# Ordering the first group's fp16 splits behind the next copy out of PSUM, and pulling one attention unit ahead of a weight transpose

## The chip, the cores and the metric

The kernel runs on 1 core of one Trainium2 chip. The metric is the device time of one execution in microseconds (us). Before the change it is 954.72 us, the median of 3 runs (952.37 to 956.6). Below, PE is TensorE, DVE is VectorE, ACT is ScalarE, POOL is GpSimd, SP is SyncE.

## What is computed

A decaying linear attention, then a gated block without an activation function, then a mixture of 8 experts in which each token goes to its two best ones:

```
for t in range(S):                                # B, H, S, D = 4, 8, 768, 48
    state = alpha[t][:, None] * state + outer(k[t], v[t])
    y[t]  = q[t] @ state
x   = y as 3072 tokens x 384
h   = ((x @ w1) * (x @ w2)) @ w3                  # 384 -> 1024 -> 1024
x   = h @ w_out                                   # 1024 -> 384
logits = x @ w_gate + log1p(exp(x @ w_noise)) * noise
out = sum over the top 2 experts e of  weight * (relu(x @ ew1[e]) @ ew2[e])
```

All of it is float32 in and out.

## The kernel before

Tokens are handled in 8 groups of G = 384 (three blocks of 128). Large products are done in fp16 with each float32 operand cut into a high and a low half by `split`: ACT writes `hi` (line 180), then DVE or POOL writes `lo = src - hi` (lines 182 and 184); three matmuls (high times high, high times low, low times high) stand for one.

**Stages.** Attention is a list of small units (`att_units`): `prep_*` (transposes of q, k, alpha and their scaling, lines 219 to 246), `scores` (L299), the masking of the scores (L316), `mix` (L342 and L353: query times state, scores times v), `ktok` (L330), `state` (L374 to L386), `xturn` (L407, with the copy L408 into `xT`). The gated block and the weights are another list (`mix_units`): `wide` (L541 to L543) makes one block of 128 columns of x@w1 (i = 0) or x@w2 (i = 1) in PSUM; ACT copies it out as `ab0` or `ab1` (L545); after the second, DVE multiplies the two (L551) and `split` makes `gh` and `gl`. `narrow` (L570 to L572) multiplies those by the 1024 x 400 matrix W = w3 @ [w_out, w_out@gates]. W itself is made during the first group, by `fuse_units`: for each of 8 row blocks of w_out, `fuse_out_turn` (three transposes, L482, and ACT's copy `woT`, L484) and `fuse_out` (L490); then for 16 half blocks of w3, `fuse_turn` (four transposes, L499, split into `w3h` and `w3l`) and `fuse_mul` (twelve matmuls, L510 to L512). Weights come as 64-bit words that `conversions` turns into float32 on DVE and ACT (L422, L424, L427).

After attention come routing (`rank`) and the experts (L922 to L934). Weights of the first experts are prepared beside the last `wide` and `narrow` units: `EARLY` lists how many preparing steps go behind each unit that is left once attention has ended.

**What sets the order.** PE's order is written out by the main loop: it emits one attention unit, adds its cost to `ta`, and then emits units of the other list as long as their summed cost `tm` stays under a limit that grows with `ta`. Each unit of both lists carries a cost, in estimated us. On the other engines a scheduler orders the instructions; `tc.issue_after(i)` makes an instruction stand behind instruction `i`. The engines then take their own instructions strictly in the order of their queue.

For groups 1 to 7 and blocks f < 7, the split of a gated block isn't emitted at once: it is kept in `AB["rest"]`, and at the next `wide` it is emitted with `behind=copied.ins`, so that ACT's `gh` stands behind the next copy `ab`. In group 0, and for f = 7, it is emitted at once.

Of the kernel before, what the change touches and what calls it, by code (L numbers as in the profile page):

```python
# [13 lines left out]
AF = mybir.ActivationFunctionType  # L14
# [12 lines left out]
NF = F // P  # L27
# [17 lines left out]
RG = 6  # L45
WB = 12
WU = 3
WP = 3
TA = 30
CS = 2.6  # L50
# [9 lines left out]
PGL = range(4)  # L60
# [21 lines left out]
def body(ctx, tc, q, k, v, alpha, mw1, mw2, mw3, mwo, wg, wn, noise, ew1, ew2, out, dbg=None):  # L82
    nc = tc.nc
# [92 lines left out]
    def split(src, hi, lo, scale=None, engine=None, behind=None):  # L176
        with ExitStack() as st:
            if behind is not None:
                st.enter_context(tc.issue_after(behind))
            nc.scalar.activation(hi, src, AF.Copy, scale=1.0 if scale is None else scale)  # L180
        if scale is None:
            (engine or nc.vector).tensor_tensor(lo, src, hi, OP.subtract)  # L182
        else:
            nc.vector.scalar_tensor_tensor(lo, src, scale, hi, op0=OP.mult, op1=OP.subtract)  # L184
# [20 lines left out]
    def bank(*shape, dt=F32):  # L205

        t = ps.tile([P, PB], F32, name="ps")
        if dt != F32:
            t = t.bitcast(dt)
        n = 1  # L210
        for x in shape:
            n *= x
        t = t[:, :n]
        return t if len(shape) == 1 else t.rearrange("p (a b) -> p a b", a=shape[0])
# [218 lines left out]
    FT, FO, FS = {}, {}, {}  # L433
# [44 lines left out]
    def fuse_out_turn(f):  # L478
        wo = FS.pop(f)
        tr = bank(NK, P)  # L480
        for kk in range(NK):
            nc.tensor.transpose(tr[:, kk, :], wo[:, kk * P:(kk + 1) * P], ident)  # L482
        FO[f] = stg.tile([P, NK, P], F32, name="woT")
        nc.scalar.activation(FO[f], tr, AF.Copy)  # L484

    def fuse_out(f):
        woT = FO.pop(f)
        pr = bank(2 * E)
        for kk in range(NK):
            nc.tensor.matmul(pr, woT[:, kk, :], wr[:, kk, :], start=kk == 0, stop=kk == NK - 1)  # L490
        split(pr, woh[:, f, DM:], wol[:, f, DM:], SW)

    def fuse_turn(f, hf):
        s = FS.pop((f, hf))
        th = stg.tile([P, 4, P], F16, name="w3h", bufs=3)
        tl = stg.tile([P, 4, P], F16, name="w3l", bufs=3)
        tr = bank(4, P)
        for j in range(4):
            nc.tensor.transpose(tr[:, j, :], s[:, j * P:(j + 1) * P], ident)  # L499
        split(tr, th, tl, SW)  # L500
        FT[f, hf] = (th, tl)

    def fuse_mul(f, hf):
        th, tl = FT.pop((f, hf))
        if hf == 0:
            FT[f] = bank(W)
        pw = FT[f]
        for j in range(4):
            kk = 4 * hf + j
            nc.tensor.matmul(pw, th[:, j, :], woh[:, kk, :], start=kk == 0, stop=False)  # L510
            nc.tensor.matmul(pw, th[:, j, :], wol[:, kk, :], start=False, stop=False)
            nc.tensor.matmul(pw, tl[:, j, :], woh[:, kk, :], start=False, stop=kk == NF - 1)  # L512
        if hf:
            split(FT.pop(f), Wf[0][:, f], Wf[1][:, f], 1.0 / SW)
# [3 lines left out]
    GS, AB, X2, RT, LAST = {}, {}, {}, {}, []  # L518
# [13 lines left out]
    def wide(g, f, i, c1=G):  # L532

        xT = XT[g]
        fs = slice(f * P, (f + 1) * P)
        c0 = GS.get((g, f, i), 0)
        GS[g, f, i] = c1
        cs, n = slice(c0, c1), c1 - c0
        pm = bank(n)
        for kk in range(NK):  # L540
            nc.tensor.matmul(pm, wab[i][0][:, kk, fs], xT[:, kk, cs], start=kk == 0, stop=False)  # L541
            nc.tensor.matmul(pm, wab[i][0][:, kk, fs], xT[:, NK + kk, cs], start=False, stop=False)  # L542
            nc.tensor.matmul(pm, wab[i][1][:, kk, fs], xT[:, kk, cs], start=False, stop=kk == NK - 1)  # L543
        a = gp.tile([P, G], F32, name=f"ab{i}")[:, :n]
        copied = nc.scalar.activation(a, pm, AF.Copy, scale=SG if i == 0 else 1.0)  # L545
        if "rest" in AB:
            split(*AB.pop("rest"), behind=copied.ins)
        AB[i] = a
        if i:
            a = AB[0]  # L550
            nc.vector.tensor_tensor(a, AB[1], a, OP.mult)  # L551
            if c0 == 0:
                GS[g, f] = [gp.tile([P, G], F16, name=x, bufs=10) for x in ("gh", "gl")]
            gh, gl = GS[g, f]
            if 0 < g and f < NF - 1:
                AB["rest"] = (a, gh, gl)
            else:
                split(a, gh[:, cs], gl[:, cs], engine=nc.gpsimd if g == 0 and f in PGL else None)

    def narrow(g, t, part):  # L560
        ts = slice(t * P, (t + 1) * P)
# [219 lines left out]
    def fuse_units():  # L781

        n0 = 4 * NK
        yield 0.33, (lambda: fuse_out_turn(0)), n0 + 1
        for f in range(NF - 1):
            yield 0.33, (lambda f=f: fuse_out_turn(f + 1)), n0 + f + 2
            yield 0.55, (lambda f=f: fuse_out(f)), 0
        n0 += NF
        seq = [(f, hf) for f in range(NF) for hf in range(2)]
        yield 0.45, (lambda: fuse_turn(*seq[0])), n0 + 1  # L790
        yield 0.55, (lambda: fuse_out(NF - 1)), 0
        for n, x in enumerate(seq):
            if n + 1 < len(seq):
                yield 0.45, (lambda n=n: fuse_turn(*seq[n + 1])), n0 + n + 2
            yield 2.05, (lambda x=x: fuse_mul(*x)), 0
# [16 lines left out]
    def mix_units():  # L812
        fu = fuse_units()
        for g in range(NG):
            for f in range(NF):
                for i in range(2):
                    if g == 0:
                        yield (0.0, (lambda f=f: convert((f // 4 + 1) * 2 * NK + AH)), TG - 1)
                    yield (1.48, (lambda g=g, f=f, i=i: wide(g, f, i)), (g + 1) * TG - 1)
                    if g == 0 and f >= FF:  # L820
                        c, x, n = next(fu)
                        yield 0.0, (lambda n=n: convert(n + AH)), 0
                        yield c, x, 0
                if f == (RF if g == NG - 1 else RG) and g:
                    yield (0.1, (lambda g=g: LAST.append(rank(g - 1))), 0)
                if g == NG - 1 and 0 <= f - NF + NTP[0] < NTP[0]:
                    yield (0.0, (lambda t=f - NF + NTP[0]: turn_part(0, 0, t)), 0)
            if g == 0:
                for c, x, n in fu:
                    yield 0.0, (lambda n=n: convert(n + AH)), 0  # L830
                    yield c, x, 0
                yield (0.0, end_of_weights, 0)
            for t in range(TG):
                for part in range(2):
                    yield (2.05, (lambda g=g, t=t, part=part: narrow(g, t, part)), 0)
# [352 lines left out]
    def warm(n):  # L1188

        pm = bank(HF) if n else None  # L1190
        for _ in range(n):
            nc.tensor.matmul(pm, ident16, idle, start=True, stop=True)
# [5 lines left out]
    with tc.manual_schedule(engines={mybir.EngineType.PE}):  # L1198
# [4 lines left out]
        for c, f in att_units():  # L1203
            turned = set(done)
            f()
            ready |= turned
            ta += c
            if MS not in done:
                t0 = ta
                dve = [i for i in nc.cur_bb.bb.instructions[-40:] if i.engine == mybir.EngineType.DVE]  # L1210
                marks += dve[-1:]
                if marks:
                    with tc.issue_after(marks[max(0, len(marks) - LAG)]):
                        convert(int(CR * (ta - CS)))
                if c and 0 in done and nconv >= 2 * NK and pieces:
                    wide(0, *pieces.pop(0), P)
                elif c:
                    warm(WP if ta < 4.1 else WU)
                continue
            while nxt is not None and nxt[2] in ready | {0} and tm < RATIO * (min(ta, TK) - t0) + R2 * max(ta - TK, 0.0):  # L1220
                nxt[1]()
                tm += nxt[0]
                nxt = next(M, None)
# [42 lines left out]
```

## Time and profile before

| | |
|---|---|
| time, median of 3 runs | 954.72 us (952.37 to 956.6) |
| time of the profiled execution | 952.11 us |
| its span | 950.4 us |
| PE busy | 915.6 us (96%) |
| PE weight loads busy | 602.1 us (63%) |
| DVE busy | 621.2 us (65%) |
| ACT busy | 449.4 us (47%) |
| POOL busy | 255.6 us (27%) |
| mean granted PE clock | 0.983 of full speed |

The span is the stretch from the first to the last instruction on the chip; the execution's time is 1.7 us longer. Busy shares are averages over stages of different kinds: the first 200 us hold the weights and the first group, the attention runs to 482 us (last L407), the experts from 529.4 us (first L922). The clock row of the page tells in tenths what part of PE's full speed was granted in each of 40 slices of 23.8 us.

### The profile page before, as it was taken

Reading aid. Unit: us, or ns where it says so; the run is one execution under the profiler, and the core shown is the slowest. Engines: PE = TensorE matmul, PEld = TensorE weight load, DVE = VectorE, ACT = ScalarE, POOL = GpSimd, SP = SyncE. Lnnn points to the kernel's source line nnn. Section 1 sums busy time; section 2 is a strip of 40 time slices with the busy share of each in tenths; the row PEclk is TensorE's granted clock in tenths of the full one; section 3 lists DMA queues with packets and bytes.
Section 4 is the critical chain, followed back from the end, with each engine's and each line's share of the span. In section 5 each row is a group of like instructions: output and inputs, shape, how many; then the busy total and the mean of one; then the engine's idle time right before and its main releaser. Section 6 shows DMA issues by size and latency. Waiting matters only on the chain.

```text
span 950.4 us, 17655 instructions
## 1 busy us (share of the span) xinstructions
PE 915.6 (96%) x6823; PEld 602.1 (63%) x6823; DVE 621.2 (65%) x1705; ACT 449.4 (47%) x908; POOL 255.6 (27%) x246
## 2 busy tenths in 40 slices
PE   7889999999999999999999999999999999999996
PEld 4667777777766666676665456656656565656563
DVE  6988878577879798696878836636272635545220
ACT  2676666363565655645555432334342524334321
POOL 1211110003141231415052162542323242333213
PEclk9979799999999999999999999999999999999999
DMA  9889672242405344101137267975857565776313
GB/s 241 230 151 137 162 186 64 42 84 80 96 15 115 42 108 60 65 4 44 59 111 148 92 125 177 188 153 142 142 123 155 120 153 100 173 127 136 37 11 45
DMA packets 189269, 105.54 MB, mean 111 GB/s; under 512 B 156912, under 2 KB 174912, under 8 KB 189184
## 3 DMA queue, kind: packets, MB, share of 16 engines
q1 hardware_dynamic: 172624, 68.04, 33.9%
q0 software_dynamic: 16560, 36.37, 17.9%
q8 instruction: 54, 0.88, 0.4%
q14 instruction: 31, 0.25, 0.1%
HBM read 73.06 MB, written 20.31 MB: 98 GB/s over the span
## 4 chain that ended last, share of the span: by engine, by line
PE 69%; DVE 19%; ACT 6%; issue 3%; DMA 1%; another core or an unknown queue 0%; POOL 0%; POOLq 0%; DVEq 0%; ACTq 0%; SPq 0%
PE ps L922 7%; PE ps L932 7%; PE ps L924 6%; PE ps L923 6%; PE ps L933 6%; PE ps L934 6%; PE ps L541 3%; PE ps L543 3%; PE ps L542 3%; PE ps L353 2%; PE ps L570 2%; PE ps L572 2%; PE ps L571 2%; PE ps L299 2%; DVE Gx L235 1%
## 5 line engine op out<-in xcount | busy, mean ns | idle before, releaser
L926 DVE SCALAR_TENSOR_TENSOR hl<-ps,hh 128x512 f16<-128x512 f32 (+1 forms) x128 | 74.2, 587 | 101.6 <-ACT hh L925 101.1
L923 PE MATMUL ps<-xT,eh 128*128 128x320 f16 (+1 forms) x384 | 130.3, 339 | 0.0
L924 PE MATMUL ps<-xT,el 128*128 128x320 f16 (+1 forms) x384 | 130.3, 339 | 0.0
L922 PE MATMUL ps<-xT,eh 128*128 128x320 f16 (+1 forms) x384 | 130.3, 339 | 0.0
L958 POOL DMA_INDIRECT out_dram<-ysb,mt x56 | 86.9, 1551 | 154.4 <-ACT ysb L955 152.6
L933 PE MATMUL ps<-el,hh 128*128 128x384 f16 x384 | 125.3, 326 | 0.0
L934 PE MATMUL ps<-eh,hl 128*128 128x384 f16 x384 | 125.3, 326 | 0.0
L932 PE MATMUL ps<-eh,hh 128*128 128x384 f16 x384 | 125.3, 326 | 0.0
L925 ACT ACTIVATE hh<-ps 128x512 f16<-128x512 f32 (+1 forms) x128 | 65.6, 516 | 101.8 <-PE ps L924 92.4
L955 ACT ACTIVATE ysb<-ps,wv 128x384 f32<-128x384 f32 (+1 forms) x56 | 32.4, 578 | 142.1 <-PE ps L934 80.3
L184 DVE SCALAR_TENSOR_TENSOR el<-es,esc,eh 128x512 f16<-128x512 f32 (+1 forms) x80 | 67.1, 856 | 43.5 <-ACT eh L180 37.4
L700 POOL DMA_INDIRECT table<-md,ad x48 | 50.8, 1058 | 155.4 <-DVE ad L697 127.2
L910 POOL DMA_INDIRECT xg<-x2s,mt x56 | 54.9, 981 | 104.6 <-DMA mt<-table 67.5
L545 ACT ACTIVATE ab<-ps 128x384 f32<-128x384 f32 (+2 forms) x136 | 62.9, 470 | 38.2 <-PE ps L543 20.2
L182 POOL TENSOR_TENSOR sm<-sf,sm 128x512 f16<-128x512 f32 x24 | 29.9, 1272 | 154.2 <-ACT sm L180 154.2
L541 PE MATMUL ps<-xT,w1h 128*128 128x384 f16 (+2 forms) x204 | 65.1, 321 | 1.0 <-DVE Kt L246 0.6
L570 PE MATMUL ps<-Wh,gh 128*128 128x400 f16 x192 | 63.9, 333 | 1.8 <-ACT gh L180 1.5
L541 PE MATMUL ps<-xT,w0h 128*128 128x384 f16 (+2 forms) x204 | 64.6, 319 | 1.1 <-ACT xT L408 1.1
L543 PE MATMUL ps<-xT,w1l 128*128 128x384 f16 (+2 forms) x204 | 65.1, 320 | 0.2 <-DVE w1l L184 0.2
L542 PE MATMUL ps<-xT,w1h 128*128 128x384 f16 (+2 forms) x204 | 65.1, 320 | 0.0
L543 PE MATMUL ps<-xT,w0l 128*128 128x384 f16 (+2 forms) x204 | 64.6, 319 | 0.0
L542 PE MATMUL ps<-xT,w0h 128*128 128x384 f16 (+2 forms) x204 | 64.5, 318 | 0.0
(288 smaller groups left out, 2072.9 us busy)
## 6 DMA issues: line engine op xcount, KB each, us to landing
es<-in_moe_w_dram SPq DMA_DIRECT2D x32, 768.0 KB
s<-in_moe_w_dram POOLq DMA_DIRECT2D x16, 512.0 KB
out_dram<-zero POOLq DMA_DIRECT2D x5, 960.0 KB
v<-in_v_dram SPq DMA_DIRECT2D x24, 192.0 KB
x2s<-xr SPq DMA_DIRECT2D x24, 192.0 KB
pad<-in_alpha_dram SPq DMA_DIRECT2D x21, 192.0 KB
pad<-in_q_dram SPq DMA_DIRECT2D x21, 192.0 KB
pad<-in_k_dram SPq DMA_DIRECT2D x21, 192.0 KB
```

What stands on the lines that cost most here:

```text
L541: nc.tensor.matmul(pm, wab[i][0][:, kk, fs], xT[:, kk, cs], start=kk == 0, stop=False)
L542: nc.tensor.matmul(pm, wab[i][0][:, kk, fs], xT[:, NK + kk, cs], start=False, stop=False)
L543: nc.tensor.matmul(pm, wab[i][1][:, kk, fs], xT[:, kk, cs], start=False, stop=kk == NK - 1)
L570: nc.tensor.matmul(pm, gh[:, ts], Wf[0][:, f], start=f == 0, stop=False)
L922: nc.tensor.matmul(pm, w1h[:, kk, fs], xT[:, kk, :n], start=kk == 0, stop=False)
L923: nc.tensor.matmul(pm, w1h[:, kk, fs], xT[:, NK + kk, :n], start=False, stop=False)
L924: nc.tensor.matmul(pm, w1l[:, kk, fs], xT[:, kk, :n], start=False, stop=kk == NK - 1)
L926: nc.vector.scalar_tensor_tensor(hl[:, f], pm, 0.0, hh[:, f], op0=OP.max, op1=OP.subtract)
L932: nc.tensor.matmul(py[:n], hh[:, f, ts], w2h[:, f], start=f == 0, stop=False)
L933: nc.tensor.matmul(py[:n], hh[:, f, ts], w2l[:, f], start=False, stop=False)
L934: nc.tensor.matmul(py[:n], hl[:, f, ts], w2h[:, f], start=False, stop=f == NF - 1)
L958: i = nc.gpsimd.indirect_dma_start(out=out, out_offset=bass.IndirectOffsetOnAxis(ap=mt[:n, t, 0:1].bitcast(U32), axis=0), in_=ys[:n], in_o ...
```

## The change

The split of every gated block is now kept, group 0 included, together with the engine for its low half. A new function `gated` emits it; it is called behind `wide`'s copies as before, and newly behind `fuse_out_turn`'s copy `woT`. For f = 7 of the groups 1 to 7 it is still emitted at once. And in `fuse_units`, ahead of the second `fuse_turn`, an empty unit of cost `PULL` = 2.5 is put in: it raises `tm` without emitting anything, so that the main loop emits more attention before it goes on with that list, there and at all later points.

```diff
@@ constants
 WU = 3
+PULL = 2.5
 WP = 3
@@ fuse_out_turn(f)
         FO[f] = stg.tile([P, NK, P], F32, name="woT")
-        nc.scalar.activation(FO[f], tr, AF.Copy)
+        gated(nc.scalar.activation(FO[f], tr, AF.Copy).ins)
@@ wide(g, f, i, c1)
         copied = nc.scalar.activation(a, pm, AF.Copy, scale=SG if i == 0 else 1.0)
-        if "rest" in AB:
-            split(*AB.pop("rest"), behind=copied.ins)
+        gated(copied.ins)
         AB[i] = a
...
             gh, gl = GS[g, f]
-            if 0 < g and f < NF - 1:
-                AB["rest"] = (a, gh, gl)
-            else:
-                split(a, gh[:, cs], gl[:, cs], engine=nc.gpsimd if g == 0 and f in PGL else None)
+            AB["rest"] = (a, gh[:, cs], gl[:, cs], None, nc.gpsimd if g == 0 and f in PGL else None)
+            if 0 < g and f == NF - 1:
+                gated()
+
+    def gated(behind=None):
+        if "rest" in AB:
+            split(*AB.pop("rest"), behind=behind)
@@ fuse_units()
         for n, x in enumerate(seq):
+            if n == 0:
+                yield PULL, (lambda: None), 0
             if n + 1 < len(seq):
                 yield 0.45, (lambda n=n: fuse_turn(*seq[n + 1])), n0 + n + 2
```

How the instructions move is shown at three places. The line numbers of the changed kernel are 1 to 5 higher.

ACT, at the end of the first group's `wide` units; before:

```order
L180 ACTIVATE woh<-ps 128x16
L545 ACTIVATE ab_1348<-ps 128x384
L180 ACTIVATE gh<-ab_1321 128x384
L484 ACTIVATE woT<-ps 128x384
L228 ACTIVATE A_1381<-ps 128x3x128
```

and now:

```order
L181 ACTIVATE woh<-ps 128x16
L546 ACTIVATE ab_1348<-ps 128x384
L485 ACTIVATE woT<-ps 128x384
L181 ACTIVATE gh<-ab_1321 128x384
L229 ACTIVATE A_1381<-ps 128x3x128
```

The high half `gh` of the last gated block (f = 7) and the copy `woT` have changed places. Seven more `gh` of the group have moved in the same way, behind the next copy.

PE, where the first half blocks of w3 are transposed (L499, in the changed kernel L500); before:

```order
L482 MATMUL ps<-ident,s_1290 128x128 x3
L490 MATMUL ps<-wr,woT 128x16 x3
L299 MATMUL ps<-Qt,Kt 128x128 x8
L499 MATMUL ps<-ident,s_1367 128x128 x4
L490 MATMUL ps<-wr,woT 128x16 x3
L499 MATMUL ps<-ident,s_1409 128x128 x4
L510 LDWEIGHTS w3h
```

and now:

```order
L483 MATMUL ps<-ident,s_1288 128x128 x3
L491 MATMUL ps<-wr,woT 128x16 x3
L300 MATMUL ps<-Qt,Kt 128x128 x8
L500 MATMUL ps<-ident,s_1365 128x128 x4
L491 MATMUL ps<-wr,woT 128x16 x3
L343 MATMUL ps<-Zs_119,Qt 128x96 x4
L354 MATMUL ps<-v,sm 128x48 x8
L500 MATMUL ps<-ident,s_1409 128x128 x4
L511 LDWEIGHTS w3h
```

One `mix` (L343 and L354) now stands between the first and the second transposes of w3; before, it stood behind the second ones and the twelve matmuls of the first half block.

DVE, at the same place (L316 and L317 mask scores, L184 and L185 make the low half `w3l`); before:

```order
L316 TENSOR_TENSOR sm<-ps,causal 128x512
L427 SCALAR_TENSOR_TENSOR s_1441<-s_1439,keep,s_1441 128x512
L184 SCALAR_TENSOR_TENSOR w3l<-ps,w3h 128x512
L184 SCALAR_TENSOR_TENSOR wol<-ps,woh 128x16
L422 TENSOR_SCALAR s_1462<-s_1460 128x512
```

and now:

```order
L317 TENSOR_TENSOR sm<-ps,causal 128x512
L428 SCALAR_TENSOR_TENSOR s_1441<-s_1439,keep,s_1441 128x512
L317 TENSOR_TENSOR sm<-ps,causal 128x512
L185 SCALAR_TENSOR_TENSOR w3l<-ps,w3h 128x512
L185 SCALAR_TENSOR_TENSOR wol<-ps,woh 128x16
```

The second masking of the scores, which stood eight places further down, is now ahead of the first `w3l`.

## Rows read from the trace of the kernel before

**Rows 1.** The page: span, PE's line, and PE's granted clock by slices

```profile
span 950.4 us, 17655 instructions
...
PE 915.6 (96%) x6823; PEld 602.1 (63%) x6823; DVE 621.2 (65%) x1705; ACT 449.4 (47%) x908; POOL 255.6 (27%) x246
...
PEclk9979799999999999999999999999999999999999
```

**Rows 2.** PE's waits, 100 to 120 us: waiter, releaser, us in total, times, longest

```profile
PE ps L490 <- ACT woT L484: 1.0, 1, 1.0
PE ps L512 <- DVE w3l L184: 0.8, 1, 0.8
```

**Rows 3.** Stretches: length, busy us of PE, PEld, DVE, ACT, POOL, granted clock, DMA

```profile
102.86:106.27 3.41, 2.45 (x30) 2.08 (x27) 3.41 (x10) 2.80 (x7) 0.53 (x1) 1.00 1.05 171
106.27:116.51 10.24, 9.42 (x40) 6.98 (x38) 7.22 (x16) 5.96 (x8) 2.11 (x4) 0.50 0.65 197
```

**Rows 4.** ACT's waits, 60 to 108 us

```profile
ACT gh L180 <- DVE ab L551: 7.2, 4, 3.2
```

**Rows 5.** ACT in order of time: start, us, instruction, idle before and its releaser

```profile
103.47 0.52 ACT L180 ACTIVATE gh<-ab 128x384 f16<-128x384 f32 x1 [2.05 <-DVE ab L551]
103.90 0.47 ACT L484 ACTIVATE woT<-ps 128x384 f32<-128x384 f32 x1
...
105.52 0.52 ACT L484 ACTIVATE woT<-ps 128x384 f32<-128x384 f32 x1
```

**Rows 6.** PE in order of time, 104 to 118 us

```profile
104.43 0.84 PE L490 MATMUL ps<-wr,woT 128*128 128x16 f32 x6 [0.96 <-ACT woT L484]
105.20 1.16 PE L299 MATMUL ps<-Qt,Kt 48*128 48x128 f32 x16
106.29 1.11 PE L499 MATMUL ps<-ident,s 128*128 128x128 f32 x4
...
110.92 0.52 PE L512 MATMUL ps<-woh,w3l 128*128 128x400 f16 x1 [0.82 <-DVE w3l L184]
...
114.22 1.86 PE L342 MATMUL ps<-Zs,Qt 112*128 112x96 f32 x8
...
117.93 0.62 PE L499 MATMUL ps<-ident,s 128*128 128x128 f32 x4
```

**Rows 7.** PE in order of time, the same kinds of work at full clock

```profile
118.39 0.33 PE L510 MATMUL ps<-woh,w3h 128*128 128x400 f16 x1
...
120.42 0.60 PE L499 MATMUL ps<-ident,s 128*128 128x128 f32 x4
...
137.31 1.03 PE L342 MATMUL ps<-Zs,Qt 112*128 112x96 f32 x8
...
139.93 0.62 PE L499 MATMUL ps<-ident,s 128*128 128x128 f32 x4
```

**Rows 8.** DVE in order of time, 103 to 118 us

```profile
103.93 0.68 DVE L246 TENSOR_TENSOR Kt<-ps,Gx 128x384 f32<-128x384 f32 x1
...
107.31 0.75 DVE L427 SCALAR_TENSOR_TENSOR s<-s,keep,s 128x512 int32<-128x512 int32 x1 [0.30 <-ACT woh L180]
...
110.17 0.69 DVE L184 SCALAR_TENSOR_TENSOR w3l<-ps,w3h 128x512 f16<-128x512 f32 x1
...
112.77 0.75 DVE L427 SCALAR_TENSOR_TENSOR s<-s,keep,s 128x512 int32<-128x512 int32 x1
...
117.91 0.69 DVE L316 TENSOR_TENSOR sm<-ps,causal 128x512 f32<-128x512 f32 x1 [2.89 <-PE ps L353]
```

**Rows 9.** An earlier fall of the clock: part of a mix

```profile
51.83 3.54 PE L353 MATMUL ps<-v,sm 128*128 128x48 f32 x16
```

**Rows 10.** The stretch 52 to 56 us, columns as in Rows 3

```profile
52.00:56.00 4.00, 4.00 (x25) 4.00 (x25) 4.00 (x9) 2.08 (x5) 1.57 (x3) 0.50 1.35 229
```

**Rows 11.** PE's waits, 120 to 600 us

```profile
PE ps L299 <- DVE Kt L246: 1.8, 3, 0.8
...
PE ps L889 <- DVE em L884: 0.4, 1, 0.4
```

## The prediction

> **What bounds the kernel now.** I read the page first. PE is busy 915.6 of the span's 950.4 us, so it sets the end, and what can be won is PE's idle time, 34.8 us in all, and stretches in which its clock is at the lower level [rows 1]. The clock row shows three dips in the first eighth of the span and none later until the very end [rows 1]. The time of this execution is 952.11 us, 2.6 below the median of the runs, 954.72; I make the sum against 952.11 and carry the difference over to the median.
>
> The change touches two places that matter to PE, both between 100 and 120 us, so next I asked what PE waits for there. There are two waits: 1.0 us for ACT's copy `woT`, and 0.8 us for the low half `w3l` from DVE [rows 2]. [...]
>
> **Why `woT` was late.** ACT takes its queue in order. Between 60 and 108 us it stood 7.2 us in front of four `gh`, waiting for DVE's product `ab` [rows 4]. The last of these is the one that costs PE time: `gh` of block 7 stands ahead of `woT`, waits 2.05 us and runs at 103.47; `woT` follows at 103.90, and PE's L490, which reads it, starts at 104.43 after 0.96 us idle [rows 5, 6]. The other three cost PE nothing that a wait in the trace shows.
>
> **Part 1, `gh` behind the next copy.** No instruction is added or removed. With `woT` ahead of that `gh`, it is done before 103.47, and L490 can start when PE is free, 104.43 - 0.96 = 103.47. Then the next thing is late: the eight score matmuls L299 write two banks, and by the order of banks these are the ones that DVE's L246 for Qt and Kt empties, Kt at 103.93 + 0.68 = 104.61 [rows 8]. L490 takes 105.20 - 104.43 = 0.77 [rows 6], so PE would be there at 104.24: a new wait of up to 0.37. For the other seven moved `gh` I take nothing: ACT is then waiting for a PE copy instead of for DVE, and POOL's low halves come a copy later (0.5 us, the `woT` row [rows 5]) with their reader, `narrow`, more than 60 us away. If that cover were wrong, the cost is bounded by a few copies of 0.5 us.
>
> **Part 2, the pulled unit.** It adds nothing to PE either: one `mix` goes from behind the first twelve w3 matmuls to ahead of the second transposes. What it changes is whom PE waits for. While the mix runs, ACT and DVE can make `w3h` and `w3l`, which PE waited for at 110.92 [rows 6]. But on DVE the second masking of the scores now stands ahead of the first `w3l`, and that masking needs a buffer that the mix frees: before, it ran at 117.91, right at the mix's end [rows 8]. So the wait for `w3l` isn't gone, it gets a new reason.
>
> **The sum.** Work from L490 to the end of that mix and the first twelve matmuls, at full clock: L490 0.77 and scores 106.29 - 105.20 = 1.09 [rows 6]; two transposes, 118.39 - 117.93 = 0.46 each [rows 6, 7]; a second L490, 0.77; twelve matmuls, 120.42 - 118.39 = 2.03; a mix, 139.93 - 137.31 = 2.62 [rows 7]. Together 8.20. Before, the same work took from 103.47 to 117.93, 14.46. The excess is 6.26: 0.96 and 0.82 of waits, and 4.48 for the clock.
>
> [...]
>
> With the change I expect PE to reach 105.7 at the scores' end (104.61 + 1.09), 106.2 after the first transposes, 106.9 after L490, 109.55 after the mix, 110.0 after the second transposes. DVE's first `w3l` started at 110.17; one masking ahead of it (0.69) puts it at 110.85 and its end at 111.54, or 0.3 earlier if DVE's wait at 107.31 for ACT goes [rows 8]. PE wants it two matmuls after 110.0, at 110.3. So the wait is between 0.2 (if DVE gains more) and 1.2; I take 1.0, nearest to the row of `w3l`. New total: 8.20 + 0.37 + 1.0 = 9.6, if the clock stays up. Gain 14.46 - 9.6 = 4.9 us.
>
> Does the clock stay up? That is the largest term and no row decides it. [...] I take it as likelier than not.
>
> **Later.** The empty unit's cost stays in `tm`, so attention runs about one unit ahead of the other list to its end. Some transposes and `rank`s change place in every later group; the number of instructions on each engine is the same. PE's waits there are of 0.3 to 0.8 us; for Kt, three, 1.8 in total, longest 0.8 [rows 11]. I take no net change, bounded by seven groups times 0.8 = 5.6 either way. When attention ends, two more units are left than before, and the steps of the first experts' weights come as many units earlier against them; the first such step had PE wait 0.4 us for DVE's `em` [rows 11], and from the last transposes to that step there is one `wide` and three parts of `narrow` in place of four parts, some 0.5 us less. So 0.5 lost. On SP, one transpose of gathered tokens goes ahead of two writes of group 6, on POOL one output goes ahead of three gathers; no PE wait in the trace follows from either, so zero, at most the 0.5 of a single issue.
>
> Forecast: 952.11 - 4.9 + 0.5 = 947.7 for an execution like the profiled one, 954.72 - 4.4 = **950.3** for the median.
>
> **Rivals.**
>
> *The clock falls all the same.* Then only the waits go: 0.96 - 0.37 + 0.82 = 1.4, less 0.5 at the experts: 953.8. It speaks for it that the pulled mix itself doesn't bring the clock up: from 52 to 56 us PE was fully busy, mostly with a mix (3.54 us), and the clock stayed at 0.50 [rows 9, 10]. With the mix wholly in the slow stretch, another 2.62 us of work would be doubled: up to 956.4.
>
> *Conversion becomes the bound.* PE comes to w3 some 5 us earlier, but the converted blocks come from a chain of load, DVE, ACT, DVE. The fourth block's last step began at 112.77 [rows 8], PE would want it about 115.5. If loads are later by 2 us, PE waits at each transpose and gives the gain back: 954 to 955.
>
> *More waits for buffers later (slower).* Place: the transposes of q and k in groups 1 to 7 that now stand six or nine in a row; DVE empties a bank in 0.68 us, and where PE gets there first it waits, as at L299. From one more wait of the longest size (0.8) in each group on, it costs 5.6. With the clock's gain absent: 954.7 - 0.9 + 5.6 = 959.4 and, with the last masking late too (0.69), 960. Against it: as many rows of transposes are taken apart as are put together.
>
> *More than forecast.* Neither new wait arises (1.4 more) and a wait or two later goes (0.5 to 1.5): 947 to 949.
>
> *It doesn't do what it says.* The order shows that it does; the rest of this case is that `gh` was not what held `woT`, and lies within the first rival.
>
> **How the numbers follow.** A measurement of this kernel can tell some 0.5% from no change, 4.8 us: below 949.9 is faster, above 959.5 slower. Forecast (949 to 952): 0.38, of which some 0.4 lies below 949.9. More than forecast: 0.20. The clock falls: 0.22. Conversion: 0.08. Slower: 0.12. Faster is 0.20 + 0.15 = 0.35, the same 0.53, slower 0.12. The likeliest case's own range is 949 to 952. The range 945.5 to 957.0 takes in the first rival's upper end and the fourth's lower with an added later wait or two; it leaves out the slower case and a little at the bottom.
>
> **What would show it.** In the changed profile: no idle time of L491 for ACT; `woT` ahead of `gh` on ACT; the granted clock at 1.00 between 100 and 120 us, or a shorter dip; the first low-half matmul (L513) waiting up to 1 us behind the mix; PE's waits after 120 us no more than a few us different from before. It would be wrong if the dip is as long as before, if PE waits for DVE's conversions (L428) at several transposes, or if waits for Kt and `ys` in the later groups grow by 3 us or more.

## The result and the profile after

The change makes the kernel slower: 963.44 us (median, 962.08 to 964.98) against 954.72 (952.37 to 956.6), 5 runs of each, a ratio of 1.0088 with a 95% interval of 1.0062 to 1.0115. The prediction was 950.3 us with a range of 945.5 to 957.0. Two unedited copies (runs 9 and 14) gave 1.0112 [1.0081, 1.0144] and 1.0086 [1.0052, 1.0121].

The page of the changed kernel (its profiled execution took 963.44 us) answers to [rows 1]:

```profile
span 961.7 us, 17667 instructions
...
PE 919.5 (96%) x6823; PEld 604.8 (63%) x6823; DVE 622.6 (65%) x1705; ACT 448.5 (47%) x908; POOL 254.2 (26%) x246
...
PEclk9779999999999999999999999999999999999998
```

The span is 11.3 us longer: 3.9 of it is PE's busy time, 7.4 its idle time. The busy time grows with the same 6823 matmuls, and the granted clock is lower (0.979 against 0.983). PE's order moves, so equal times from the start hold different work. I cut both spans at the same events instead: w3's first transposes, the first `narrow` of groups 0, 2, 3 and 6, the first expert's first matmul, and the second expert's. These are PE's stretches so cut, in order; columns are the stretch, its length, PE's busy us, granted clock, DMA share and GB/s. Idle time is length less busy. First the kernel before:

```profile
0.00:106.29 106.29, 90.24 (x695) 0.92 0.86 182
106.29:168.96 62.67, 61.18 (x429) 0.92 0.52 138
168.96:274.63 105.67, 105.38 (x820) 1.00 0.32 66
274.63:326.91 52.28, 50.81 (x423) 1.00 0.41 77
326.91:479.69 152.78, 148.56 (x1252) 1.00 0.23 57
479.69:529.59 49.90, 48.71 (x299) 1.00 0.62 144
529.59:576.43 46.84, 46.84 (x245) 1.00 0.53 108
576.43:950.39 373.96, 363.92 (x2678) 0.99 0.61 122
```

The changed kernel, cut at the same events:

```profile
0.00:107.76 107.76, 93.97 (x695) 0.87 0.83 178
107.76:171.47 63.71, 59.40 (x453) 1.00 0.58 147
171.47:277.02 105.55, 103.97 (x796) 1.00 0.29 62
277.02:332.24 55.22, 53.00 (x419) 0.97 0.38 73
332.24:484.96 152.72, 147.85 (x1255) 1.00 0.24 61
484.96:537.93 52.97, 50.25 (x295) 0.97 0.53 122
537.93:587.64 49.71, 47.17 (x245) 1.00 0.43 88
587.64:961.72 374.08, 363.93 (x2677) 0.99 0.60 124
```

Line by line: the first three stretches together are 2.4 us longer (277.02 - 274.63). In the second the clock is now 1.00 instead of 0.92, as predicted, and still nothing is gained: idle time there went from 1.49 to 4.31 us. (24 more matmuls lie in it too, as many as a mix has, which the third stretch then lacks: it has 1.4 us less of busy time and 1.3 more of idle time.) Group 2 to 3, the fourth stretch, is 2.9 longer; the opening of the experts, the sixth and seventh, 3.1 and 2.9 longer. The rest is level. So **the gain is gone by the first `narrow` of group 2, and two later places cost 9 us**.

PE's waits from 100 to 945 us in the changed kernel (waiter, releaser, us in total, times, longest). In them `em` is the greatest value of a block of an expert's weights, from which its scale is made, `hl` the low half of an expert's hidden layer, and `xT`, read by L927, the first expert's tokens, gathered as `xg` and transposed by a DMA:

```profile
PE ps L300 <- DVE Kt L247: 6.3, 5, 2.5
PE ps L894 <- DVE em L889: 2.5, 2, 2.3
PE ps L513 <- DVE w3l L185: 1.7, 2, 1.3
PE ps L939 <- DVE hl L931: 1.6, 1, 1.6
...
PE ps L927 <- DMA xT<-xg: 0.9, 1, 0.9
```

Before, Kt cost 1.8 us in this stretch, em 0.9, and hl and xT nothing. Two of the longer waits are followed by the lower clock level: in PE's order of time,

```profile
312.37 0.49 PE L300 MATMUL ps<-Qt,Kt 48*128 48x128 f32 x4 [1.71 <-DVE Kt L247]
...
517.64 0.19 PE L894 MATMUL ps<-em,part 128*128 128x1 bf16 x1 [2.29 <-DVE em L889]
```

and directly behind each the stretch is at 0.50 (columns as before):

```profile
312.90:316.31 3.41, 3.41 (x12) 0.50 0.73 83
517.70:521.11 3.41, 3.41 (x12) 0.50 0.33 77
```

Each costs some 1.7 us, half its length, by an estimate from the rows: PE is busy throughout (3.41 of 3.41 us), and its matmuls of 128x384 (L542 to L544) start 0.32 us apart there, where at 307 us they start 0.16 apart. The fall at 312 comes with the lead: all ten profiles of kernels that keep it until there have one between 310 and 315 us, and none of the other eight has.

### The profile page after: what moved, and what is told of

It reads as the page before. It is cut to its first block, busy times and chain, and to the rows that moved or that the text cites. A ratio compares the mean times of both kernels' runs of the same rounds, so it can differ in the third digit from the quotient of the medians.

```text
span 961.7 us, 17667 instructions
## 1 busy us (share of the span) xinstructions
PE 919.5 (96%) x6823; PEld 604.8 (63%) x6823; DVE 622.6 (65%) x1705; ACT 448.5 (47%) x908; POOL 254.2 (26%) x246
## 2 busy tenths in 40 slices
DMA packets 189269, 105.54 MB, mean 110 GB/s; under 512 B 156912, under 2 KB 174912, under 8 KB 189184
## 4 chain that ended last, share of the span: by engine, by line
PE 62%; DVE 23%; ACT 6%; issue 4%; DMA 2%; SPq 1%; POOL 1%; POOLq 0%; DVEq 0%; ACTq 0%
PE ps L937 6%; PE ps L939 6%; PE ps L938 6%; PE ps L927 5%; PE ps L929 5%; PE ps L928 5%; PE ps L542 3%; PE ps L543 3%; PE ps L544 3%; PE ps L575 2%; PE ps L573 2%; PE ps L574 2%; PE ps L354 2%; DVE esc L886 2%; PE ps L300 2%
## 5 line engine op out<-in xcount | busy, mean ns | idle before, releaser
L927 PE MATMUL ps<-xT,eh 128*128 128x320 f16 (+1 forms) x384 | 130.2, 339 | 1.0 <-DMA xT<-xg 0.9
L185 DVE SCALAR_TENSOR_TENSOR el<-es,esc,eh 128x512 f16<-128x512 f32 (+1 forms) x80 | 66.7, 855 | 51.7 <-ACT eh L181 42.5
L542 PE MATMUL ps<-xT,w0h 128*128 128x384 f16 (+2 forms) x204 | 65.7, 324 | 0.9 <-ACT xT L409 0.9
L542 PE MATMUL ps<-xT,w1h 128*128 128x384 f16 (+2 forms) x204 | 66.5, 326 | 0.0
L543 PE MATMUL ps<-xT,w1h 128*128 128x384 f16 (+2 forms) x204 | 66.5, 326 | 0.0
L544 PE MATMUL ps<-xT,w1l 128*128 128x384 f16 (+2 forms) x204 | 66.4, 326 | 0.0
L543 PE MATMUL ps<-xT,w0h 128*128 128x384 f16 (+2 forms) x204 | 65.7, 324 | 0.3 <-issue 0.3
L544 PE MATMUL ps<-xT,w0l 128*128 128x384 f16 (+2 forms) x204 | 65.6, 323 | 0.0
```

Source lines behind the costliest of these rows:

```text
L927: nc.tensor.matmul(pm, w1h[:, kk, fs], xT[:, kk, :n], start=kk == 0, stop=False)
```

## The experiments

Sixteen kernels ran, in four sets of four; the kernel before, run beside them in each set, had medians of 952.89, 949.66, 954.54 and 954.96, on three chips (the last two sets on one), so ratios are what to compare. **Theory A** at the start: the loss comes from attention running one unit ahead to its end, and the gating is harmless. **Theory B**: the gating disturbs the copies. **C**: the falls of the clock in the first 70 us differ between executions whatever the kernel.

**1. Gating alone.** The change without the pulled unit:

```diff
-            if n == 0:
-                yield PULL, (lambda: None), 0
```

> The splits of the first group stand behind the next copy, but the empty unit (PULL) is left out; PE's order is that of the kernel before. Theory A (the loss comes from attention running one unit ahead to its end, and the gating is harmless): 952 to 955 us, ratio 0.998 to 1.001, PE's wait for woT near 104 us gone or under 0.4. Theory B (the gating itself disturbs the first 70 us, where the changed kernel shows 27 us at the lower clock against 17 before): 958 to 960 us, with 27 us at the lower clock there. Theory C (the dips of the first 70 us differ from execution to execution whatever the kernel): time as in A, while the length at the lower clock there is anything from 17 to 27 us.

954.18 us, ratio 1.0013 [0.9992, 1.0034]. PE's wait for `woT` at 104 is gone. The wait for w3l stays (1.01), w3's transposes wait 1.37 for a converted block, and the clock falls at 108.8 for 6.8 us. Gating alone neither gains nor loses. C holds as well: before 100 us this profile has 20.5 us at the lower clock, that of run 2 has 17.1.

**2. The pulled unit alone.** The kernel before with the three lines of `PULL`, no other line of the change.

> The empty unit alone, splits as in the kernel before; PE's order is that of the changed kernel. Theory A: 962 to 965 us, with PE waiting about 2 us for em near 517 us and for hl and xT near 559 and 588 us. Theory B: 957 to 959 us, since only the part of the loss that isn't from the first 70 us stays. Theory C: 962 to 965 us.

964.88 us, ratio 1.0123 [1.0094, 1.0153]. The whole loss is there without the gating: B falls, and A stands. The clock falls at 105.5 for 13.7 us.

**3. The unit returned.** The changed kernel, with the lead taken back when the fused weights are done; PE's order is that of before from group 0's first `narrow` on:

```diff
             yield 2.05, (lambda x=x: fuse_mul(*x)), 0
+        yield -PULL, (lambda: None), 0
```

> The whole change, with a unit of cost -PULL behind the last unit of the weights' list: the mix still goes ahead of w3's second transposes, but from the first narrow of group 0 on PE's order is that of the kernel before. Theory A: the losses after 170 us are gone and the gain at 104 to 118 us stays: 949 to 953 us. Theory B: 955 to 958 us. If the waits after 170 us came from the order of DVE and ACT and not from PE's order: 960 us or more.

953.35 us, ratio 1.0004 [0.9984, 1.0023]. The lead is the loss. But the expected gain isn't there either. Its trace shows where that goes. From w3's first transposes to its third it is 3.8 us ahead of the kernel before, to the ninth 1.7, to the first `narrow` of group 2 0.8; and the opening of the experts, where em waits 2.17 us, is 1.7 longer (51.64 against 49.90). The largest loss is a wait for Kt. DVE, in order of time, then PE, in run 3:

```profile
122.84 0.75 DVE L428 SCALAR_TENSOR_TENSOR s<-s,keep,s 128x512 int32<-128x512 int32 x1 [1.46 <-ACT s L425]
...
127.04 0.66 DVE L247 TENSOR_TENSOR Kt<-ps,Gx 128x384 f32<-128x384 f32 x1
```

```profile
111.98 0.34 PE L513 MATMUL ps<-woh,w3l 128*128 128x400 f16 x1 [1.26 <-DVE w3l L185]
...
124.36 0.94 PE L300 MATMUL ps<-Qt,Kt 48*128 48x128 f32 x12
127.76 0.49 PE L300 MATMUL ps<-Qt,Kt 48*128 48x128 f32 x4 [2.46 <-DVE Kt L247]
130.22 0.60 PE L500 MATMUL ps<-ident,s 128*128 128x128 f32 x4
```

The same scores in the kernel before, with its Kt:

```profile
130.23 0.61 PE L499 MATMUL ps<-ident,s 128*128 128x128 f32 x4
130.77 0.94 PE L299 MATMUL ps<-Qt,Kt 48*128 48x128 f32 x12
132.38 0.49 PE L299 MATMUL ps<-Qt,Kt 48*128 48x128 f32 x4 [0.67 <-DVE Kt L246]
```

```profile
131.65 0.67 DVE L246 TENSOR_TENSOR Kt<-ps,Gx 128x384 f32<-128x384 f32 x1
```

With a later wait of 0.48 for w3l, run 3 stands 4.2 us here, against 1.5 before (0.82 and 0.67). Count from w3's first transposes (105.81 in run 3, 106.29 before). DVE has Kt after 21.9 us instead of 26.0, so 4.1 sooner; but PE asks for it 5.9 sooner, after 19.5 instead of 25.4. Of this 2.5 us is what it is ahead by then, and 3.4 is the order: one attention unit ahead, these scores stand in front of w3's seventh transposes (130.22), where before they stood behind them (130.23). So the pulled unit itself brings a part of this wait: it is 0.68 in run 1, without the pull, and 0.98 and 1.95 in runs 2 and 7 (below), which have the pull and not the gain (0.4 behind and 0.8 ahead of before at the third transposes). On DVE, ahead of Kt, 1.46 us go in a wait for ACT's conversion step; run 12 asks what that costs.

**4. The list of steps shifted.** The changed kernel; attention ends with two more units left than before, so `EARLY` gets two more zeros:

```diff
-EARLY = (0, 3, 0, 6, 0, 0, 0, 1, ...
+EARLY = (0, 0, 0, 3, 0, 6, 0, 0, 0, 1, ...
```

> The whole change, with two zeros put ahead of EARLY, so that the preparing steps of the experts' weights keep their places against the end of the other list (two units more are left than before). Theory A in its narrow form (what costs is that the steps now come two units earlier against PE's remaining work): PE's wait for em near 517 us falls from 2.3 to under 0.6 us and the dip of the clock behind it goes, 958 to 960 us. If instead the waits spread over the groups 1 to 6 carry the loss: 962 to 965 us.

956.25 us, ratio 1.0026 [1.0007, 1.0045], somewhat better than was expected. The waits for hl and xT are gone, em costs 0.2, the clock doesn't fall at 517. Its stretches that answer to the fourth, sixth and seventh above:

```profile
276.80:332.04 55.24, 52.96 (x420) 0.97 0.38 73
...
484.42:534.84 50.42, 48.55 (x294) 1.00 0.59 129
534.84:581.62 46.78, 46.78 (x245) 1.00 0.53 108
```

The opening is back within 0.5 us of before (49.90 and 46.84); group 2 to 3 still costs its 3 us.

**Why em is late at all.** In the changed kernel SP takes one transpose of gathered tokens ahead of group 6's writes `x2s` (blocks of its output, from the buffers `xr`), and the transpose stands for its gather, whose signals the trace has from 502.20 to 502.27, until 502.40 (SPq are SP's issues of DMAs):

```profile
502.40 1.32 SPq L921 DMA_TRANSPOSE xT<-xg  x1
503.83 1.00 SPq L600 DMA_DIRECT2D x2s<-xr  x2
504.91 5.48 SPq L921 DMA_TRANSPOSE xT<-xg  x3
```

ACT's third block of group 6 needs the buffer of the first write, as there are two (the row names no releaser; in run 6 below the same instruction waits 2.01 us for that write):

```profile
507.21 0.61 ACT L181 ACTIVATE xr<-x,am 128x384 f16<-128x384 f32 x1 [4.95 <-issue]
```

and everything behind it on ACT and DVE, em among it, is some 4 us later. That is **theory S**, the order on SP. But there was something else. (A signal is an update of a semaphore, from which the profile tells who waits for whom.) The trace's semaphore records show no signal of PE between 503.73 and 509.96, though by PE's rows four matmuls that signal end in that time; then four signals come 0.10 us apart. **Theory T**: signals come late near the transposes. PE's rows run on through that stretch, with those four ends from 504.66 to 509.04, and nothing in them shows the delay.

**5. The four transposes held back** behind a late copy of ACT (`touch` writes one column of `xT` from `ab1`):

```diff
-                if g == NG - 1 and 0 <= f - NF + NTP[0] < NTP[0]:
-                    yield (0.0, (lambda t=f - NF + NTP[0]: turn_part(0, 0, t)), 0)
+                if g == NG - 1 and f == NF - 2:
+                    for t in range(NTP[0]):
+                        yield (0.0, (lambda t=t: (touch(0, 0, t), turn_part(0, 0, t))), 0)
```

> The changed kernel, with the four transposes of the first expert's gathered tokens held back until ScalarE has copied the second to last block of the last group's wide layer (a copy of one column each makes them wait): they then start near 513 us instead of 502 and lie behind all three writes of group 6's blocks and behind the maximum em. Theory S (the order on SP: one transpose ahead of two writes, whose landing ScalarE and VectorE wait for, 4.95 and 3.92 us in the changed kernel) and theory T (whatever waits for a signal of another engine near these transposes gets it some us late: a TensorE end of 503.19 was signalled at 509.96) both expect: no ScalarE wait over 3 us from 498 to 512, the wait of L894 for em at 517 falls from 2.29 us to under 0.5, no half-clock stretch at 517, median 957 to 960 (after: 963.4). If the four transposes come too late for the first expert, its first matmul waits up to 3 us and the gain is as much smaller. A theory by which the wait for em comes from the order of attention alone expects 963 and the wait as it was.

963.7 us, ratio 1.0152 [1.0125, 1.0178]. The em that was late at 517 waits no more, as expected. But the transposes started at 519, not 513, and loads of weights stand behind them on SP, from 524.49: the next em was 3.01 us late, at 534.30, with the clock down for 3.4 us behind it. A miss: one late DMA was traded for another.

**6. The writes first.** The transposes are ordered behind all three writes, no later than that:

```diff
+    def turn_after(t):
+        with tc.issue_after(X2["write"]):
+            turn_part(0, 0, t)
```

> The changed kernel, with the transposes of the first expert's tokens ordered on SP behind all three writes of group 6's blocks, otherwise as early as they can be. Theory S expects the whole remedy: wait for em under 0.5 us, no half-clock stretch at 517, median 957 to 960. Theory T expects part of it or nothing: the transposes then start near 503 to 505, signals come late from there to some 512, the wait for em stays between 1 and 2.5 us, the half-clock stretch at 517 stays where that wait is over 1 us, median 961 to 964.

958.71 us, ratio 1.0106 [1.0078, 1.0134]. In the profile em waits at most 0.2 us and the clock stays up at 517; the waits for hl and xT stay (1.6 each). Yet the ratio is that of the unedited change in other sets; no copy of it ran beside this one. In none of the four runs of this set was a signal late.

**7. The pull and its return without gating**, in the kernel before.

> The kernel before, with the attention unit in front of w3's second transposes and returned at the end of the fused weights (the order of TensorE is that of the third run, but no gated split in the first group). If gating is what lets woT come ahead of gh, the wait for woT at 104 stays near 1 us, the wait for w3l is gone, and the clock may fall there for 3.4 to 10 us or not at all: median 952 to 956. If gating itself costs something later (the wait for em of 2.17 us in the third run against 0.42 before), this run keeps the wait at 0.4 and comes out 0.5 to 2 us below the third run (953.35).

952.64 us, ratio 1.0028 [1.0010, 1.0046]. The wait for `woT` is 1.0 us, and the clock falls at 107.6 for 10.2 us. So it takes both parts to keep the clock up there.

**8. Unit returned and transposes held back** (3 and 5 together).

> The third run's kernel (gating, one attention unit in front of w3's second transposes and returned at the end of the fused weights) with the transposes held back as in the first kernel of this call. Theories S and T: the wait for em falls from 2.17 us to under 0.5, the other gains of the third run stay (1.3 us at the second narrow block), median 951 to 952.5 beside 953.35, if the transposes are in time for the first expert. It would be the fastest so far. The theory that the order of attention alone sets the wait for em: 953 to 954.

951.51 us, ratio 1.0023 [1.0006, 1.0041]: no wait for em over 0.2, and no gain.

**9. The change again**, unedited.

> The changed kernel, unedited, beside the others of this call, since the median of the kernel before has moved between the calls (954.7, 952.9, 949.7). Ratio to the kernel before of 1.009 to 1.014; wait for em above 1 us and a half-clock stretch at 517 if these belong to the kernel and not to one execution.

964.77 us, ratio 1.0112 [1.0081, 1.0144]. em waits 2.71 us, and the clock falls at 313.2 and 518.0 as in the first profile: both belong to the kernel.

**10. List shifted and writes first** (4 and 6).

> The changed kernel with both late losses mended: the list of the first experts' steps shifted by two zeros, as in the fourth run, and the four transposes behind the three writes of group 6, as in the sixth. If the lead of attention costs only there, this comes out level with the kernel before: ratio 0.998 to 1.002. If the waits of the groups between (Kt, Zs, 300 to 375 us) are the kernel's own, some 3 us stay: ratio 1.003 to 1.006. Waits for em, hl and xT all under 0.5 us in both.

958.42 us, ratio 1.0045 [1.0025, 1.0066]: the waits of the groups between are the kernel's own. em 0.43, hl and xT none. PE's signals were late again (none from 503.30 to 507.63), although the transposes began at 508.27.

**11. Unit returned and writes first** (3 and 6).

> The third run's kernel (gating, one attention unit ahead and returned at the end of the fused weights) with the four transposes behind the writes: the wait for em falls from 2.17 us to under 0.5 and nothing else changes. 1.5 to 2 us below the third run's 1.0004: ratio 0.997 to 0.9995. If the transposes are now late for the first expert, a wait for xT of up to 1.6 us takes it back.

955.45 us, ratio 1.0001 [0.9982, 1.0021]; em waited 2.23 us all the same, a miss, and it refutes T as I had put it. ACT stands 4.35 us for a signal of PE, and SP has issued only a load and the writes; the transposes come 5 us later:

```profile
506.69 0.49 ACT L546 ACTIVATE ab<-ps 128x384 f32<-128x384 f32 x1 [4.35 <-PE ps L544]
```

```profile
501.16 0.38 SPq L884 DMA_DIRECT2D es<-in_moe_w_dram  x1
501.81 9.78 SPq L600 DMA_DIRECT2D x2s<-xr  x3
511.68 5.96 SPq L922 DMA_TRANSPOSE xT<-xg  x4
```

**12. The middle step of converting w3 on DVE**, on top of 11:

```diff
-            s = to_float32(got[n], m, n >= NVB)
+            s = to_float32(got[n], m, NVB <= n < 4 * NK + NF)
```

> The run before this one, with the middle step of converting w3's blocks on VectorE in place of ScalarE (an operation of 0.73 to 0.86 us on VectorE in the first blocks). VectorE now stands up to 1.5 us at a time, 8.0 us in all from 100 to 170 us, for ScalarE's step. Theory: the gain of 4 us at 118 us is given back by 140 because Kt stands behind these steps on VectorE, which waits for ScalarE in them. Then Kt's wait at 127 falls from 2.46 us to under 1.5 and the lead of 4 us over the kernel before at the third transposes of w3 is 2 us or more at the ninth; ratio 0.994 to 0.999. Rival: VectorE's work itself is the bound there (10 of 12 us busy from 118 to 130); with some 0.75 us more for each of 16 blocks the waits stay or grow, ratio 0.999 to 1.006.

955.63 us, ratio 1.0007 [0.9989, 1.0025]. Kt's wait is 2.09 in place of 2.46, and the 4.0 us by which it is ahead of before at the third transposes are 0.3 at the ninth. Run 11, without this edit, has nothing left there, and run 3 has 1.7: in runs 11 and 12 the clock falls behind the wait for Kt, which costs the 1.7, and in run 3 it doesn't. So the edit itself is worth 0.3 us at the ninth. It doesn't tell what ACT's step costs, as it puts work on DVE for the wait that it takes away. From 112 to 128 us (length, DVE's busy us, then as before), in run 3 and in run 12:

```profile
112.00:128.00 16.00, 12.79 (x29) 1.00 0.67 192
```

```profile
112.00:128.00 16.00, 15.86 (x34) 0.98 0.71 181
```

In run 12 DVE's own work is the bound, the rival in the expectation.

**13 to 16, one chip.** Open were whether late signals belong to the change, and how the loss divides. 13 is the kernel before, unedited:

> The kernel before, unedited, for a second profile on the chip of this call. If late signals between 485 and 520 us (a TensorE end whose signal is recorded over 2 us later) come with the chip or the execution and not with the change, they show here too where the two runs after this one show them, and the wait for em is 0.2 to 2.2 us. If they belong to the change, they stay at the 2.0 us of the first profile or less, with em at 0.4. Ratio 0.998 to 1.002.

955.77 us, ratio 1.0007 [0.9984, 1.0029]. Signals are late here too: PE's were silent for 4.67 us, with three ends in them, against 2.92 in the first profile of this kernel; em waits 1.2 us against 0.42. They are not the change's.

14 is the change, unedited:

> The changed kernel, unedited, on the same chip as the other three. Ratio 1.009 to 1.012. With late signals: wait for em over 2 us and a half-clock stretch at 517 us. Without: wait for em under 1 us, no such stretch, and the ratio nearer to 1.006.

962.88 us, ratio 1.0086 [1.0052, 1.0121]; em 2.0, hl 1.6, xT 1.6, the clock down at 313.5 and 518.3.

15 is run 6 again:

> The sixth run's kernel on a chip of which a profile of the kernel unedited exists. If the order of SP's queue is what makes em late, em waits under 0.5 us here while the kernel unedited waits over 2 us, and this is 3 to 4.5 us faster than it. If it was the chip of that call, em waits as long as in the kernel unedited, or short in both, and the two are within 1.5 us.

962.11 us, ratio 1.0079 [1.0055, 1.0103]. em waits 0.9 where run 14 waits 2.0, the clock stays up at 517, and the opening up to the first expert's first matmul is 2.2 us shorter (50.96 against 53.20). The medians differ by 0.8, inside both intervals. So S shows in one pair of profiles, less than was expected of it, and its worth in the median, 0 to 3 us, stays unresolved.

16 keeps the lead through groups 1 to 4 and returns it behind group 4's `narrow`, so that PE's order is that of before from group 5's last units on:

```diff
                     yield (2.05, (lambda g=g, t=t, part=part: narrow(g, t, part)), 0)
+            if g == 4:
+                yield (-PULL, lambda: None, 0)
```

> The changed kernel, with the attention unit returned behind group 4's narrow layer: the lead is kept from w3's second transposes through groups 1 to 4, and TensorE's order is that of the kernel before from group 5's wide layer on, the opening of the experts included. Theory: of the 9 to 11 us, 6 to 8 come from the opening of the experts (wait for em, half-clock stretch, waits for hl and xT) and 3 from the waits at 300 to 375 us that the lead brings (Zs 0.4, Kt 1.7 and 1.0, half-clock stretch at 312). Then this is 1.002 to 1.005, with those waits still there and those for hl and xT gone. Rival: the lead costs only at the opening: 0.998 to 1.001.

960.02 us, ratio 1.0051 [1.0034, 1.0068]. About half the loss is there although PE's order at the opening is that of before. Its stretches, in the same places as for run 4:

```profile
274.61:329.63 55.02, 52.96 (x421) 0.97 0.38 73
...
482.62:535.18 52.56, 50.04 (x301) 0.97 0.54 136
535.18:581.96 46.78, 46.78 (x246) 1.00 0.53 108
```

That is 2.7 us for group 2 to 3, none for hl and xT, and 2.7 for em (a wait of 2.3, and the clock down at 518.2), which with this order waits 2.1 to 2.2 in runs 1, 3, 11 and 12 as well, all with late signals, and 0.2 in 7 and 8, without them. (Unedited, the kernel before waits 0.42 and 1.2 with late signals; whether gating adds to it there stays open.)

**No version beat the kernel before**; 1, 3, 11 and 12 are level with it. Returning the lead sooner than in run 3, right behind w3's second transposes, was not tried.

## Why the prediction was wrong

*Right: what held `woT`, and the clock.* In the changed kernel `woT` runs at 104.16, ahead of the `gh` that stood in front of it in [rows 5]:

```profile
104.16 0.49 ACT L485 ACTIVATE woT<-ps 128x384 f32<-128x384 f32 x1 [0.49 <-PE ps L483]
...
106.07 0.53 ACT L181 ACTIVATE gh<-ab 128x384 f16<-128x384 f32 x1 [1.43 <-DVE ab L551]
```

and PE has no wait there. From 100 to 118 us the clock is at 1.00, where [rows 3] had 10.24 us at 0.50:

```profile
100.00:118.00 18.00, 16.73 (x140) 1.00 0.55 142
```

In all thirteen profiles with both parts it stayed up there; in the five with one part or none (before, runs 1, 2, 7 and 13) it fell. The rival "the clock falls all the same" is out for this stretch; near 130 us, behind the wait for Kt, it falls in six of the thirteen. (The prediction read three dips from the clock row of [rows 1]; that row shows two lowered slices.)

*Right in size: the sum of the stretch.* Predicted 9.6 us from L490 to the third transposes, with 1.0 for w3l: measured 115.62 - 105.54 = 10.1, with 1.26:

```profile
105.54 0.74 PE L491 MATMUL ps<-wr,woT 128*128 128x16 f32 x6
...
113.92 0.34 PE L513 MATMUL ps<-woh,w3l 128*128 128x400 f16 x1 [1.26 <-DVE w3l L185]
...
115.62 0.60 PE L500 MATMUL ps<-ident,s 128*128 128x128 f32 x4
```

The 0.37 for Kt didn't show, and the work without the wait took 8.8 us, not 8.20, so some of the agreement is luck. Gain 14.46 - 10.1 = 4.4 instead of 4.9.

*Wrong, first: that this gain lasts, and that the pulled unit "adds nothing to PE".* The sum ended at the third transposes, and what PE would meet next wasn't costed. One attention unit ahead, PE also comes to the next scores one half block of w3 sooner, and waits 2.46 us for Kt in run 3 and in the change, where it waited 0.67; in six of thirteen profiles the clock falls behind that wait, for another 1.7. Of the 3.8 us gained since the first transposes, run 3, without such a fall, has 1.7 left at the ninth. The rival "conversion becomes the bound" (0.08) came near it, the gain given back to DVE's queue, but at another place: PE waits once, at the scores, and not at each transpose, and DVE's longest wait for a load there is 0.7 (run 3). How much of it DVE's share in the conversion makes isn't settled by run 12.

*Wrong, second: "no net change, bounded by seven groups times 0.8".* The bound took the longest wait that was there as the longest that could come. With one attention unit ahead, PE waits 1.71 for Kt at 312.37, and the clock falls behind it, which no term held: 2.9 us in that stretch in the change, 2.7 in run 16, nothing in run 3 (52.22 in place of 52.28). The rival "more waits for buffers later" (0.12) was right in kind, with 959.4 to 960, though it looked for one short wait in each group and not for one long one with a fall of the clock.

*Wrong, third: "0.5 lost" at the experts' opening.* The two more units were counted right, but priced by PE's order alone: 0.5 us less between the last transposes and em. What counts is the chain of steps on ACT and DVE. Its list is tied to a count of units that begins at attention's end, so every step came two units early against PE's remaining work, and PE waits 2.29 us for em, 1.60 for hl and 0.94 for xT, with the clock down once. Cost 5.9 us; in run 4's profile two zeros in the list undo all but 0.5.

*Wrong, fourth, in the profile at least: "no PE wait follows" from the transpose ahead of the writes, "at most 0.5".* It followed through two engines: SP, the landing of the write, ACT's buffer, em. With the writes first, em waited 0.9 in place of 2.0 (runs 15 and 14). How much of the median this is stays open.

What set the late signals off isn't settled either. They appear where eight gathers, a load of 768 KB, the writes and mostly the transposes are in flight, in runs of the kernel before as well; run 11 shows that the transposes aren't needed. They were absent in the four runs of the second set, on its chip, and there in all other profiles, with 2.9 us of silence or more. Moving the gathers was not tried, and whether tracing itself has a part in it can't be told from traces.

## What to carry to other kernels

A unit moved by a planner's running sum shifts everything behind it: return the lead where its purpose ends, and look at each hand-made list that counts from an event that moved. When a wait of the bounding engine is removed, go on reading past the place: ask when it will want each next input, and when the engine that feeds it will have it. A unit pulled ahead brings the wants of all that follows it ahead as well. And compare stretches cut at the same events, not the spans.

## What the runs showed of the hardware

Near 500 us no signal of PE was recorded for up to 6.2 us while by its rows its matmuls went on and ended, and then several came 0.10 us apart (the change's first profile). A record can be missing where the signal isn't: that trace holds 770 records for 792 matmuls that signal, while in the four runs of the second set none is missing. Whether a record can be late where the signal isn't is not shown. But ACT did stand: 4.35 us in run 11 for a product that, by the order of the copies and PE's rows, had ended at 501.94. The first 100 us held 17.1 us at the lower clock in the first profile of before, 23.9 in the second; 27.3, 20.5 and 17.1 in the three of the change: of the 11.3 us between the first two spans, a part is this, and it is why one profile of each kernel can't settle 0.5%. The wait of 2.46 us for Kt near 130 us (2.09 in run 12) was followed by 3.4 us at the lower level in six of the thirteen profiles that have it, and not in the other seven.
